# Turned rows of the last two blocks made in a pair's sixth step, for pairs 0 to 10

## Chip, cores and metric

The kernel runs on one core of one Trainium2 chip. The metric is the device time of one execution in microseconds; three runs of the kernel before gave 541.6, 541.94 and 542.74, median 541.94.

## What is computed

Attention over 4 batches, 8 heads, 576 positions and a head width of 64, with rotated queries and keys, and behind it a layer of 8 experts. Each position takes one expert: its own best one, or that of the position before it when a local gate says so. The reference, cut to its core:

```python
q_rot, k_rot = rotate(q), rotate(k)
scores = np.matmul(q_rot, k_rot.transpose(0, 1, 3, 2)) / np.sqrt(D)
attn = np.exp(scores - scores.max(-1, keepdims=True))
attn = attn / (attn.sum(-1, keepdims=True) + 1e-09)
x = np.matmul(attn, v).transpose(0, 2, 1, 3).reshape(B, S, H * D)
...
logits = x @ w_gate
local_gate = 1 / (1 + np.exp(-(x @ w_local)))
# e: argmax of the logits at s == 0 or local_gate < 0.5, else the expert of s - 1
h = np.maximum(x[b, s] @ w1[e], 0.0)
out[b, s] = softmax(logits[b, s])[e] * (h @ w2[e])
```

## The kernel before

The first 300 us are attention, the rest is the experts, which the change does not touch. Attention works on 16 pairs of heads (4 batches of 4 pairs), each in nine steps; the loop over `g` runs through 16 x 9 steps. In a step, DVE takes the minimum of a score tile (`mn`, L272), PE makes the scores of the next step (`s`, L267), ACT the exponentials (`e`, L289; the tile of the last 64 rows of both heads is `et`), PE turns the tile of two steps ago with four transposes (`tm`, L325; `tk` and `tt` are the remainders), and ACT and DVE split the turned tile into a high and a low part (`pth` L303, `ptl` L307). PE multiplies these with the split values (`pv`, L361, five matmuls in most steps, ten for a result), and ACT and DVE bring the result of a half out of PSUM (`tmp`, `xt`, L371 and L372). `xt` is the attention output of a pair with positions along the columns.

`gates(p)` turns that output of pair p into rows of positions, in the steps of pair p + 2. It gives a list of functions, one of which is called per step, from a list `soon`:

- `sums`: the row sums of the exponentials and their reciprocal (L426 to L429).
- `rows(0, 3)`: three `gx` matmuls (L435) turn blocks 0 to 2 and give the gate logits with them. For pairs 0 to 10 (`POOL_ROWS` is 11) ACT copies the result to SBUF (L442), and POOL divides logits (`gm`, L448) and rows (`xrow`, L449). The store waits in a list `stores`.
- `last_rows`: `rows(3, 2)` does two `gx` matmuls for the last two blocks, and DVE divides straight from PSUM (`gm`, `xrow`, the same L448 and L449) and stores at once (L459, L463). Behind it comes the store of `rows(0, 3)`.
- after the fourth pair of a batch, `scores`: three sums that make `lg_all` (L478 to L480), on POOL for the first three batches. From `lg_all` of the first three the routing starts with `mx` and `rs` on DVE (L500, L513).

`GATES_AT` says in which step of the pair this begins: step 7 unless it names the pair, so `sums` are in step 7, `rows(0, 3)` in step 8 and `last_rows` in step 0 of the next pair. Steps count from 0.

```python
GATES_AT = {13: 4, 14: 7, 15: 4}
...
                if i == GATES_AT.get(p, 7) and p >= 2:
                    soon += gates(p - 2)
...
                if soon:
                    soon.pop(0)()
```

`ps_t` is a pool of four PSUM banks that `tm`, `tk`, `tt`, `pv` and `gx` share. `et_p` is a pool of four SBUF buffers for `et` and `xrow`.

POOL has other work: it rotates queries and keys of pair p + 2 (`stage`, L196 and L197), splits them (`xq` and `xk`, L206 the high part, L207 the low part), and splits the values (`v`, L212 and L213). For every even pair `xq` is split at full width (1152 columns) with its keys in it; for an odd one `xk` and `xq` are apart, at 576. SP issues all loads and stores. In step 0 of a pair it issues the spread of the next pair's queries and keys, twelve DMAs from `xq` and `xk` (`qtail` L234, `m` L221 to L223, `qst` L229), then the load of raw queries and keys (L189), later the stores of `xrow` and the load of values (L193).

PE's instructions keep the order in which the program writes them, from step 12 on (`MAN0`), but the scheduler of the program decides the order on DVE, ACT, POOL and SP, and in six of the later pairs the order of PE that comes of all this differs by a few matmuls from that of the others.

Of the kernel before, what the change touches and what calls it, by code (L numbers as in the profile page):

```python
# [58 lines left out]
GATES_AT = {13: 4, 14: 7, 15: 4}  # L59

SPLITS = (((1, 2, 3, 4, 5, 7), (0, 6)), ((0, 1, 3, 5, 6, 7), (5, 6)), ((3, 4, 5, 6), (1, 5, 6)), ((1, 3, 4, 7), (1, 3, 4)), ((0, 2, 4, 5, 6), (5, 6)), ((3,), (0, 7)), ((2, 5, 6, 7), (4,)))
POOL_ROWS = 11
# [75 lines left out]
def tile_attention_moe(ctx, tc, qk, v, tabs, turn, consts, tri, wg, wts, out):  # L138
# [60 lines left out]
    def rope(p):  # L199
        for f in (1, 0):  # L200
            rope_half(pool, f, qkl[:, 2 * f:2 * f + 2])
# [34 lines left out]
    def spread(p):  # L236
        spread_tail(p)
        spread_k(p)
        spread_q(p)
# [9 lines left out]
    def mm_s(g):  # L249
        p, i = tile_of(g)  # L250
        m, q = m_t[p], qst[p % 2]
        st = ps_s.tile([P, 2, 512], F32, tag="s", name=f"s_{g}")
        whole = [(h, 0, HALF, h * HALF) for h in range(2)]

        turned = [(0, 0, HALF, 64), (1, 0, 224, 64 + HALF), (1, 224, HALF, 0)]
        if i < 8:
            a, j = heads_of(i, p)
            seq = [(q[:, a, j * P:(j + 1) * P], m[:, a, c], whole) for c in range(2)]
        elif p > 1:
            qt, k = qtail[p % 2], xk[p % 2]  # L260
            seq = [(qt[:, x], k[:, y], whole) for x, y in PASSES]
        else:
            seq = [(qtail0[p][:, a], m[:, a, c], (whole, turned)[a]) for a in range(2) for c in range(2)]
        for h in range(2):
            parts_ = [(lhs, keys, lo, hi, k0) for lhs, keys, parts in seq for hh, lo, hi, k0 in parts if hh == h]
            for n, (lhs, keys, lo, hi, k0) in enumerate(parts_):
                pe.matmul(st[:, h, lo:hi], lhs, keys[:, k0:k0 + hi - lo], start=(n == 0), stop=(n == len(parts_) - 1))  # L267
        s_t[g] = st

    def softmax_min(g):  # L270
        mn = sm_p.tile([P, 1], F32, tag="mn", name=f"mn_{g}", bufs=4)
        dve.tensor_reduce(mn, s_t[g][:, :, 0:HALF], axis=AX.XY, op=ALU.min)  # L272
        return mn

    def softmax_exp(g, mn):
        p, i = tile_of(g)
        b, hp = divmod(p, NP)
        sums = sum_t[b]
        if i < 8:
            a, j = heads_of(i, p)  # L280
            if a == 0:
                e_t[p, j] = ej_p.tile([P, 2, S], F32, tag="ej", name=f"e_{p}_{j}")
            dst = e_t[p, j][:, a]
            col = (2 * hp + a) * NB + j
        else:
            e_t[p, 4] = et_p.tile([P, S], F32, tag="et", name=f"et_{p}")
            dst = e_t[p, 4]
            col = (2 * hp + 1) * NB + 4
        act.activation(  # L289
            dst.rearrange("p (h s) -> p h s", h=2), s_t.pop(g)[:, :, 0:HALF], AF.Exp,  # L290
            bias=mn, scale=-1.0, accum_out=sums[:, col:col + 1],
        )
# [90 lines left out]
    def bc(ap, axis, n):  # L383
        ap = ap.unsqueeze(axis)
        shape = list(ap.shape)
        shape[axis] = n
        return ap.to_broadcast(shape)
# [3 lines left out]
    def small(shape, tag, dt=F32, bufs=1):  # L391
        return sm_p.tile(shape, dt, tag=tag, name=f"{tag}_{next(ctr)}", bufs=bufs)
# [24 lines left out]
    def gates(p):  # L417

        b, hp = divmod(p, NP)
        heads = slice(2 * hp, 2 * hp + 2)  # L420
        if hp == 0:
            gm_t[b] = small([P, NB, H, 9], "gm")
        r = sum_t[b].rearrange("p (h j) -> p h j", j=NB)[:, heads]

        def sums():
            act.copy(r[64:128, 0, 4:5], r[0:64, 1, 4:5])  # L426
            flat = sum_t[b][:, 2 * hp * NB:(2 * hp + 2) * NB]
            act.add(flat, flat, 1e-9)
            dve.reciprocal(flat, flat)  # L429

        def rows(j0, n):
            ps = ps_t.tile([P, n, 146], F32, tag="t", name=f"gx_{p}_{j0}")
            for j in range(j0, j0 + n):
                lo = j * P if j < 4 else S - P
                pe.matmul(ps[:, j - j0], xt_t[p][:, lo:lo + P], wid[:, hp // 2, 18 * (hp % 2):18 * (hp % 2) + 146],  # L435
                          start=True, stop=True)
            rj = r[:, :, j0:j0 + n].rearrange("p a j -> p j a")
            xr = et_p.tile([P, S], F32, tag="et", name=f"xrow_{p}_{j0}")
            o, w = ((18, 0), (0, 128))[hp % 2]
            if j0 == 0 and p < POOL_ROWS:  # L440
                xr = xr[:, 0:n * 146].rearrange("p (j d) -> p j d", d=146)
                act.copy(xr, ps)  # L442
                engine, ps, xr = pool, xr, xr[:, :, o:o + P]
            else:
                engine, xr = dve, xr[:, 0:n * P].rearrange("p (j d) -> p j d", d=P)
            px = ps[:, :, o:o + P].rearrange("p j (a d) -> p j a d", d=D)
            pw = ps[:, :, w:w + 18].rearrange("p j (a e) -> p j a e", e=9)
            engine.tensor_tensor(gm_t[b][:, j0:j0 + n, heads], pw, bc(rj, 3, 9), op=ALU.mult)  # L448
            engine.tensor_tensor(xr.rearrange("p j (a d) -> p j a d", d=D), px, bc(rj, 3, D), op=ALU.mult)  # L449
            if engine is pool:  # L450
                stores.append(lambda: store(j0, n, xr))
            else:
                store(j0, n, xr)

        def store(j0, n, xr):
            t0 = 1 + b * S
            cols = slice(P * hp, P * hp + P)
            m = min(j0 + n, 4) - j0
            sp.dma_start(rows_d[t0 + j0 * P:t0 + (j0 + m) * P, cols].rearrange("(j p) d -> p j d", p=P),  # L459
                         xr[:, 0:m])  # L460
            if m < n:

                sp.dma_start(rows_d[t0 + 4 * P:t0 + S, cols], xr[64:128, m])  # L463

        stores = []

        def last_rows():
            rows(3, 2)
            for f in stores:
                f()  # L470

        return [sums, lambda: rows(0, 3), last_rows]

    def scores(b):

# [718 lines left out]
    if True:  # L1194
# [32 lines left out]
        def pv_steps(t):  # L1227
            p, i = divmod(t, 9)
            if 0 <= p < NPAIR:
                for n in range(cum[i], cum[i + 1]):  # L1230
                    pv_mm(p, n)
                    if n % 10 == 9:
                        pv_evac(p, n // 10)

        for g in range(NSTEP):
            if g == GM:
                begin.close()
            with tc.manual_schedule(engines=None if g < GM else MAN0):
                p, i = divmod(g, 9)
                if i == 0 and p % NP == 0:  # L1240
                    b = p // NP
                    sum_t[b] = sm_p.tile([P, H * NB], F32, tag="sum", name=f"sum_{b}")
                    dve.memset(sum_t[b], 1.0)
                mn = minima.pop(g) if g in minima else softmax_min(g)
                if g == 0:
                    rest_q[0]()
                if g + 1 < NSTEP:
                    mm_s(g + 1)
                softmax_exp(g, mn)
                if g < GM - 1:  # L1250
                    minima[g + 1] = softmax_min(g + 1)
                if g >= 2:
                    tr_main(g - 2)
                pv_steps(g - 11)

                if i == 0 and 2 <= p and p + 2 < NPAIR or g == SPREAD_LAST:
                    spread(p + 1)
                if g in START:
                    for f in START[g]:
                        f()  # L1260
                if i == 0 and 1 <= p and p + 2 < NPAIR:
                    rope(p + 2)
                    if p + 3 < NPAIR:
                        load_qk(p + 3)
                if i == 5 and 1 <= p and p + 3 < NPAIR:
                    split_qk(p + 2)
                if g == QK_LAST:
                    split_qk(NPAIR - 1)
                if i == 3 and 1 <= p and p + 1 < NPAIR:
                    split_v(p + 1)  # L1270
                    if p + 2 < NPAIR:
                        load_v(p + 2)

                if i == GATES_AT.get(p, 7) and p >= 2:
                    soon += gates(p - 2)
                    if (p - 2) % NP == NP - 1:
                        soon.append(lambda b=(p - 2) // NP: scores(b))
                        if (p - 2) // NP == B - 2:
                            todo += route(0, B - 1)
                if soon:  # L1280
                    soon.pop(0)()
                f = todo.pop(0) if todo else None
                if f:
                    list(f())
# [106 lines left out]
```

## Time and profile before

| what | value |
|---|---|
| median of 3 runs | 541.94 us |
| the profiled execution | 541.58 us |
| its span | 539.7 us |
| busy: PE, DVE, ACT, POOL | 96%, 71%, 64%, 63% |
| granted TensorE clock, mean | 0.994 |

The profile comes from one execution. Its span runs from the first to the last instruction, its time has 1.88 us more around that. The busy shares are means over attention and experts, so they are read by stretches. A timeline row gives an instruction's start and length; a bracket behind it gives the idle time of its engine before it and what ended that. Instructions of one engine overlap a little at their ends, so what an instruction costs is read from the start of it to the start of the next.

### The profile page before, as it was taken

The page shows a single profiled execution, that of the slowest core. Times are in us where ns is not written, and L with a number is a line of the kernel's source. Part 1 is how long each engine was busy: PE and PEld are TensorE (multiplying, and loading weights), DVE is VectorE, ACT ScalarE, POOL GpSimd, SP SyncE. Part 2 cuts the span into 40 slices and gives each one's busy share as a digit, 9 for nine tenths or more (in the row PEclk, how much of TensorE's full clock was granted, in tenths as well). Part 3 has the DMA queues.
Part 4 walks back from the last instruction along what each step waited for, and adds up shares of the span by engine and source line. Part 5 has one row for each costly group of instructions (what it writes and reads, how often), then busy time and mean ns, then how long its engine had stood idle before and what let it go on. Part 6 is the DMA issues. An engine that isn't in the chain of part 4 may idle for free.

```text
span 539.7 us, 10708 instructions
## 1 busy us (share of the span) xinstructions
PE 517.0 (96%) x3273; PEld 458.5 (85%) x3273; DVE 381.9 (71%) x703; ACT 347.2 (64%) x762; POOL 341.3 (63%) x267
## 2 busy tenths in 40 slices
PE   7989999999999999998899999999999999999993
PEld 4889999999999999997888788887888888888882
DVE  6998999999999999999999935428422637421631
ACT  4988999999999999987676523353533443532440
POOL 4998989989969989896598302337511455411332
PEclk9999999999999999999999999999999999999997
DMA  8659698887886969977278205471637496637350
GB/s 275 279 132 230 183 246 231 209 192 216 217 229 134 233 189 235 223 189 171 39 200 230 83 20 177 125 267 49 225 103 238 125 353 151 203 100 234 84 172 26
DMA packets 63611, 97.37 MB, mean 180 GB/s; under 512 B 28146, under 2 KB 38898, under 8 KB 61747
## 3 DMA queue, kind: packets, MB, share of 16 engines
q1 hardware_dynamic: 60066, 86.48, 58.1%
q0 software_dynamic: 3040, 9.71, 5.6%
q8 instruction: 28, 0.46, 0.4%
q14 instruction: 45, 0.36, 0.2%
q10 hardware_dynamic: 432, 0.36, 0.2%
HBM read 76.98 MB, written 12.86 MB: 166 GB/s over the span
## 4 chain that ended last, share of the span: by engine, by line
PE 72%; DVE 10%; POOL 5%; DMA 4%; issue 4%; ACT 3%; SPq 1%; POOLq 0%; DVEq 0%; ACTq 0%
PE h L952 18%; PE o L995 17%; PE pv L361 12%; PE s L267 10%; PE tm L325 8%; DVE mn L272 3%; PE gx L435 2%; DVE ptl L307 2%; PE th L986 2%; DMA rows_d<-xrow 2%; PE tx L938 1%; POOL stage L196 1%; PE tk L335 1%; ACT e L289 1%; DMA qst<-xq 1%
## 5 line engine op out<-in xcount | busy, mean ns | idle before, releaser
L995 PE MATMUL o<-w,hs 128*128 128x512 f32 x456 | 112.9, 397 | 0.0
L272 DVE TENSOR_REDUCE mn<-s 128x1 f32<-128x576 f32 x144 | 107.2, 744 | 2.4 <-PE s L267 0.9
L952 PE MATMUL h<-w,xs 128*128 128x512 f32 x444 | 106.1, 392 | 0.8 <-DVE xs L307 0.5
L289 ACT ACTIVATE e<-s,mn 128x576 f32<-128x576 f32 x128 | 95.4, 746 | 14.8 <-DVE mn L272 12.0
L307 DVE TENSOR_TENSOR ptl<-tm,pth 128x512 fp32r<-128x512 f32 x139 | 95.3, 686 | 12.4 <-ACT pth L303 7.4
L1001 POOL DMA_INDIRECT out_dram<-os,sidx x19 | 23.1, 1214 | 123.6 <-ACTq L903 70.3
L267 PE MATMUL s<-m,qst 128*128 128x288 f32 x512 | 95.7, 309 | 4.5 <-ACT e L289 3.0
L952 PEld LDWEIGHTS h<-w,xs 128*128 128x128 f32 x444 | 82.5, 188 | 19.1 <-DVE w L897 1.1
L995 PEld LDWEIGHTS o<-w,hs 128*128 128x128 f32 x456 | 83.0, 188 | 16.9 <-DVE hs L307 0.4
L303 ACT CAST pth<-tm 128x512 fp32r<-128x512 f32 x139 | 80.9, 582 | 12.8 <-PE tm L325 11.8
L267 PEld LDWEIGHTS s<-m,qst 128*128 128x128 f32 x512 | 74.5, 188 | 8.4 <-ACT e L289 5.3
L361 PE MATMUL pv<-pth,v 128*128 128x288 f32 x256 | 76.8, 315 | 2.4 <-DVE pkl L307 1.3
L325 PE MATMUL tm<-wid,e 128*128 128x128 f32 x512 | 77.0, 272 | 0.6 <-ACT e L289 0.5
L361 PE MATMUL pv<-ptl,v 128*128 128x288 f32 x256 | 76.5, 314 | 0.0
L196 POOL TENSOR_TENSOR stage<-stage 128x1152 f32<-128x1152 f32 x26 | 69.1, 2667 | 4.4 <-DMA stage<-in_qk_dram 4.4
L325 PEld LDWEIGHTS tm<-wid,e 128*128 128x128 f32 x512 | 62.1, 140 | 1.2 <-ACT e L289 0.7
L897 DVE TENSOR_TENSOR w<-stage,w 128x1024 fp32r<-128x1024 f32 x37 | 51.0, 1412 | 15.6 <-ACT w L894 9.8
L361 PEld LDWEIGHTS pv<-pth,v 128*128 128x128 f32 x256 | 48.2, 188 | 6.0 <-issue 3.0
L361 PEld LDWEIGHTS pv<-ptl,v 128*128 128x128 f32 x256 | 48.3, 189 | 0.0
L307 DVE TENSOR_TENSOR xs<-tx,xs 128x512 fp32r<-128x512 f32 x19 | 13.1, 688 | 44.6 <-ACTq L903 35.0
L307 DVE TENSOR_TENSOR hs<-th,hs 128x512 fp32r<-128x512 f32 x26 | 17.5, 687 | 30.6 <-ACTq L903 18.9
L197 POOL TENSOR_TENSOR stage<-stage 128x576 f32<-128x576 f32 x26 | 37.0, 1430 | 0.3
(201 smaller groups left out, 821.4 us busy)
## 6 DMA issues: line engine op xcount, KB each, us to landing
stage<-in_wts_dram SPq DMA_DIRECT2D x84, 512.0 KB
stage<-in_qk_dram SPq DMA_DIRECT2D x13, 1152.0 KB
qst<-xq SPq DMA_DIRECT2D x56, 128.0 KB
stage<-in_v_dram SPq DMA_DIRECT2D x16, 320.0 KB
m<-xq SPq DMA_DIRECT2D x14, 288.0 KB
m<-xk SPq DMA_DIRECT2D x14, 288.0 KB
m<-xq SPq DMA_DIRECT2D x14, 256.0 KB
m<-xk SPq DMA_DIRECT2D x14, 256.0 KB
```

What stands on the lines that cost most here:

```text
L196: engine.tensor_tensor(x, x, tab[:, 2 * f:2 * f + 2], op=ALU.mult)
L197: engine.tensor_tensor(rr[:, f], x[:, 0], x[:, 1], op=ALU.add)
L267: pe.matmul(st[:, h, lo:hi], lhs, keys[:, k0:k0 + hi - lo], start=(n == 0), stop=(n == len(parts_) - 1))
L272: dve.tensor_reduce(mn, s_t[g][:, :, 0:HALF], axis=AX.XY, op=ALU.min)
L289: act.activation(dst.rearrange("p (h s) -> p h s", h=2), s_t.pop(g)[:, :, 0:HALF], AF.Exp, bias=mn, scale=-1.0, accum_out=sums[:, col:col ...
L303: act.copy(hi, src)
L307: dve.tensor_tensor(lo, src, hi.bitcast(F32), op=ALU.subtract)
L325: pe.transpose(ps[:, k], src[:, k * P:(k + 1) * P], ident)
L361: pe.matmul(pv_t[p, u], lhs.rearrange("p c d -> p (c d)"), rhs, start=(n == 0), stop=(n == 9))
L897: (pool if k in on_pool else dve).tensor_tensor(lo, src, hi.bitcast(F32), op=ALU.subtract)
L952: pe.matmul(ps[:, c], xs_t[t][:, x, k], w[y][:, c * 512:(c + 1) * 512], start=(k == 0 and n == 0), stop=(k == 3 and n == 2))
L995: pe.matmul(ps, hs_t[t][:, x, k], w[y][:, (k % 2) * 512:(k % 2 + 1) * 512], start=(k == 0 and n == 0), stop=(k == 7 and n == 2))
```

## The change

`gates(p)` for pairs 0 to 10 gives another list. It begins in step 4 and not in step 7: `sums` in step 4, `rows(3, 2)` with its stores in step 5, nothing in steps 6 and 7, `rows(0, 3)` in step 8 as before, and its store in step 0 of the next pair. For the last five pairs the list holds the same three parts as before, and `GATES_AT` names the step of pairs 13 to 15, which is where gates of pairs 11 to 13 begin. The lines behind the edit move up by two (L478 becomes L476, L500 becomes L498).

```diff
@@ -464,12 +464,10 @@
 
         stores = []
 
-        def last_rows():
-            rows(3, 2)
-            for f in stores:
-                f()
-
-        return [sums, lambda: rows(0, 3), last_rows]
+        if p < POOL_ROWS:
+            rest = lambda: None
+            return [sums, lambda: rows(3, 2), rest, rest, lambda: rows(0, 3), lambda: stores[0]()]
+        return [sums, lambda: rows(0, 3), lambda: rows(3, 2)]
 
     def scores(b):
 
@@ -1271,7 +1269,7 @@
                     if p + 2 < NPAIR:
                         load_v(p + 2)
 
-                if i == GATES_AT.get(p, 7) and p >= 2:
+                if i == GATES_AT.get(p, 4) and p >= 2:
                     soon += gates(p - 2)
                     if (p - 2) % NP == NP - 1:
                         soon.append(lambda b=(p - 2) // NP: scores(b))
```

Three places of the order in which the engines get their instructions. First PE, in steps 1 to 3 of a pair of the late six (numbers behind a name tell buffers and pairs apart). Before:

```order
L267 MATMUL s_2818<-m_2470,qst_100 128x288 x4
L325 MATMUL tm_2828<-wid,et_2740 128x128 x4
L341 MATMUL tt_2835<-wid,et_2740 128x128
L267 MATMUL s_2852<-m_2470,qst_100 128x288 x4
L361 MATMUL pv_0_2841<-pth_2537,v_8_2297 128x288
```

And now:

```order
L267 MATMUL s_2818<-m_2478,qst_100 128x288 x4
L325 MATMUL tm_2828<-wid,et_2748 128x128 x4
L341 MATMUL tt_2835<-wid,et_2748 128x128
L361 MATMUL pv_0_2841<-pth_2537,v_8_2297 128x288
L361 MATMUL pv_0_2841<-ptl_2538,v_8_2297 128x288
```

The four score matmuls stood in front of the five `pv` matmuls of the new result `pv_0`; now they stand behind them.

Second, DVE. Before, in steps 0 to 2 of the same pair:

```order
L307 TENSOR_TENSOR ptl_2538<-tm_2742,pth_2537 128x4x128
L448 TENSOR_TENSOR gm_2120<-gx_3_2773,sum_1285 128x2x18
L272 TENSOR_REDUCE mn_2816<-s_2787 128x1
L307 TENSOR_TENSOR ptl_2538<-tm_2794,pth_2537 128x4x128
L307 TENSOR_TENSOR pkl_2540<-tk_2801,pkh_2539 128x256
L272 TENSOR_REDUCE mn_2850<-s_2818 128x1
L449 TENSOR_TENSOR xrow_3_2776<-gx_3_2773,sum_1285 128x256
L372 TENSOR_TENSOR xt_2584<-pv_3_2749,tmp_2585 64x288
```

And now, the one piece in step 5 of the pair before it and the other in steps 0 to 2:

```order
L307 TENSOR_TENSOR ptl_2538<-tm_2631,pth_2537 128x4x128
L372 TENSOR_TENSOR xt_2584<-pv_1_2610,tmp_2585 64x288
L448 TENSOR_TENSOR gm_2037<-gx_3_2647,sum_1293 128x2x18
L449 TENSOR_TENSOR xrow_3_2650<-gx_3_2647,sum_1293 128x256
L272 TENSOR_REDUCE mn_2687<-s_2660 128x1
```

```order
L307 TENSOR_TENSOR ptl_2538<-tm_2750,pth_2537 128x4x128
L272 TENSOR_REDUCE mn_2816<-s_2787 128x1
L307 TENSOR_TENSOR ptl_2538<-tm_2794,pth_2537 128x4x128
L307 TENSOR_TENSOR pkl_2540<-tk_2801,pkh_2539 128x256
L272 TENSOR_REDUCE mn_2850<-s_2818 128x1
L372 TENSOR_TENSOR xt_2584<-pv_3_2757,tmp_2585 64x288
```

`gm` and `xrow` of the last two blocks stood five instructions apart; now they stand next to each other, behind an `xt` addition and ahead of `mn`.

Third, POOL, in the same pair, with the rotation before and the split of values behind. Before:

```order
L196 TENSOR_TENSOR stage<-stage 128x1152
L197 TENSOR_TENSOR stage<-stage 128x576
L206 TENSOR_SCALAR xq<-stage 128x1152
L448 TENSOR_TENSOR gm_2120<-xrow_0_2726,sum_1285 128x3x18
L449 TENSOR_TENSOR xrow_0_2726<-xrow_0_2726,sum_1285 128x3x128
L207 TENSOR_TENSOR xq<-stage,xq 128x1152
L212 TENSOR_SCALAR v_9_2588<-stage 128x10x64
```

And now:

```order
L196 TENSOR_TENSOR stage<-stage 128x1152 x2
L197 TENSOR_TENSOR stage<-stage 128x576 x2
L448 TENSOR_TENSOR gm_2037<-xrow_0_2734,sum_1293 128x3x18
L449 TENSOR_TENSOR xrow_0_2734<-xrow_0_2734,sum_1293 128x3x128
L206 TENSOR_SCALAR xq<-stage 128x1152
L207 TENSOR_TENSOR xq<-stage,xq 128x1152
L212 TENSOR_SCALAR v_9_2588<-stage 128x10x64
```

`gm` and `xrow` of blocks 0 to 2 stood between the two halves of the split of `xq`; now they stand ahead of both.

On SP, the two stores of the last two blocks stood directly behind the load of raw queries and keys; now they stand behind the load of values, ahead of the next spread.

## Rows read from the trace of the kernel before

**Rows 1.** The page: busy time by engine, and the chain that ended last by engine

```profile
PE 517.0 (96%) x3273; PEld 458.5 (85%) x3273; DVE 381.9 (71%) x703; ACT 347.2 (64%) x762; POOL 341.3 (63%) x267
...
PE 72%; DVE 10%; POOL 5%; DMA 4%; issue 4%; ACT 3%; SPq 1%; POOLq 0%; DVEq 0%; ACTq 0%
```

**Rows 2.** Windows: stretch and its length, busy PE, PEld, DVE, ACT, POOL, clock, DMA

```profile
120.00:140.00 20.00, 20.00 (x160) 19.80 (x159) 18.92 (x36) 18.62 (x47) 19.74 (x18) 1.00 0.74 191
160.00:180.00 20.00, 19.87 (x157) 19.29 (x156) 17.91 (x35) 18.21 (x47) 19.10 (x15) 1.00 0.68 177
240.00:260.00 20.00, 17.65 (x136) 16.32 (x135) 19.16 (x41) 14.95 (x36) 12.00 (x15) 1.00 0.72 163
```

**Rows 3.** Timeline of PE: start, length, what; brackets show idle time before

```profile
114.22 0.69 PE L267 MATMUL s<-m,qst 128*128 128x288 f32 x4
...
130.61 0.70 PE L267 MATMUL s<-m,qst 128*128 128x288 f32 x4
...
146.99 0.70 PE L267 MATMUL s<-m,qst 128*128 128x288 f32 x4
...
161.45 0.66 PE L435 MATMUL gx<-wid,xt 128*128 128x146 f32 x4
...
163.83 0.69 PE L267 MATMUL s<-m,qst 128*128 128x288 f32 x4
```

**Rows 4.** Waits of PE's weight loads, 145 to 245 us: total, times, longest

```profile
PEld pv L361 <- issue: 2.0, 6, 0.3
...
PEld tm L325 <- DVE ptl L307: 1.2, 6, 0.2
```

**Rows 5.** Timeline of DVE: two pairs

```profile
80.34 0.42 DVE L449 TENSOR_TENSOR xrow<-gx,sum 128x256 f32<-128x256 f32 x1 [0.57 <-DMA rows_d<-xrow]
...
162.75 0.18 DVE L448 TENSOR_TENSOR gm<-gx,sum 128x36 f32<-128x36 f32 x1
...
165.35 0.42 DVE L449 TENSOR_TENSOR xrow<-gx,sum 128x256 f32<-128x256 f32 x1
```

**Rows 6.** Timeline of PE: the first score matmuls of a pair

```profile
159.72 0.79 PE L267 MATMUL s<-m,qst 128*128 128x288 f32 x4
...
176.56 0.79 PE L267 MATMUL s<-m,qst 128*128 128x288 f32 x4
...
227.03 0.79 PE L267 MATMUL s<-m,qst 128*128 128x288 f32 x4
```

**Rows 7.** Timeline of POOL

```profile
160.62 0.29 POOL L448 TENSOR_TENSOR gm<-xrow,sum 128x54 f32<-128x54 f32 x1 [3.81 <-ACT xrow L442]
...
161.78 2.68 POOL L207 TENSOR_TENSOR xq<-stage,xq 128x1152 fp32r<-128x1152 f32 x1
...
191.83 1.16 POOL L206 TENSOR_SCALAR xq<-stage 128x1152 fp32r<-128x1152 f32 x1
...
227.93 0.28 POOL L448 TENSOR_TENSOR gm<-xrow,sum 128x54 f32<-128x54 f32 x1 [0.37 <-ACT xrow L442]
...
243.96 0.58 POOL L478 TENSOR_TENSOR gm<-gm 128x180 f32<-128x180 f32 x1
...
245.05 0.27 POOL L480 TENSOR_TENSOR lg_all<-gm 128x45 f32<-128x45 f32 x1
```

**Rows 8.** Timeline of SP's DMA issues

```profile
157.44 0.54 SPq L193 DMA_DIRECT2D stage<-in_v_dram  x1
164.49 1.58 SPq L234 DMA_DIRECT2D qtail<-xq  x2
```

**Rows 9.** DMA, 164 to 178 us in 40 slices: busy share in tenths

```profile
DMA  0000040133999989899998999999899940092795
```

**Rows 10.** Timeline of DVE where the routing begins

```profile
245.42 0.69 DVE L307 TENSOR_TENSOR ptl<-tm,pth 128x512 fp32r<-128x512 f32 x1 [0.34 <-ACT pth L303]
246.02 0.27 DVE L500 TENSOR_REDUCE mx<-lg_all 128x15 f32<-128x120 f32 x1
```

## Prediction

> **What bounds the kernel now.** I read the page first [rows 1]: PE is busy 96% of the span, and 72% of the chain that ended last is PE, but 10% is DVE, 5% POOL and 4% DMA, so somewhere the chain leaves PE. The windows [rows 2] say where. From 120 to 140 us PE is busy 20.00 of 20, from 160 to 180 it is busy 19.87, with POOL at 19.10, and from 240 to 260 only 17.65, with DVE at 19.16. So there are three regimes: attention bound by PE, attention in which PE has small holes and POOL is nearly full, and a stretch after 240 that DVE bounds.
>
> Next, the length of a pair. The timeline of PE [rows 3] gives the start of the same four score matmuls in successive pairs: 114.22 to 130.61 and on to 146.99 is 16.39 a pair, 146.99 to 163.83 is 16.84. The 0.45 us more is lost once per pair in the steps around these matmuls. The table of waits of 145 to 245 us [rows 4] counts six such pairs: PE waits for DVE ptl 0.2 six times, ahead of tm, and 0.3 with no releaser six times, ahead of pv. What DVE does there [rows 5] explains it: the two gx matmuls of blocks 3 and 4 start at 161.45, DVE reads them for gm at 162.75, but for xrow only at 165.35, until 165.77. For 4.3 us one of the four PSUM banks that tm, pv and gx share is not free, the next tm waits until ptl has emptied another, and the scheduler's order puts the scores of the next step in front of five pv matmuls. One earlier pair has another fault: xrow at 80.34 waited 0.57 us for a store out of its buffer, some 0.42 of which PE lost.
>
> **The change, part by part.**
>
> *Moved matmuls.* The two gx matmuls (four passes) leave the first step of the next pair for the sixth of the same one, eleven times. PE's work is the same. Cost on PE: nothing; the xt columns that they read were finished four steps earlier.
>
> *Moved DVE work.* gm and xrow (0.18 and 0.42, [rows 5]) now stand right behind the xt addition and in front of mn, and read their bank at once. DVE does as much as before per pair. Both engines get their extra work in the same step, so nothing is hidden or uncovered; what could be new is a bank that comes free late for tm in the step behind it. Bounds for that: 0, and the 0.2 of [rows 4] in each of eleven pairs, 2.2 in all; a gain there is excluded, since nothing is taken away from that step. I take 0, because the bank is held for the length of an xt, a gm and an xrow and not for 4.3 us.
>
> *The sums.* They are written down three steps earlier, but the order of ACT keeps them in their place and DVE's reciprocal moves by a few instructions: 0, within the step's other work.
>
> *The repair.* With xrow not in step 2, the order of PE in the six pairs is again tm, tt, five pv, scores, as it is in the pairs of 16.39. Gain: 6 x 0.45 = 2.7, and 0.42 for the pair at 80 us, whose xrow buffer is now stored a pair earlier: 3.1 us on PE.
>
> *POOL.* This is where I expect it to be paid back. In every second of the late pairs POOL splits xq at full width: L206, then L207, and the spread (SP's twelve DMAs that bring keys and queries of the next pair into place) starts when L207 is done: 161.78 + 2.68 = 164.46, issue at 164.49 [rows 7, 8]. Before, L206 ran while POOL would have waited for ACT's copy of the gx rows, and gm, xrow, L207 followed. In the new order gm and xrow stand in front of both halves. gm cannot start before 0.90 us after the pair's first scores S (160.62 against 159.72, [rows 6, 7]): it waited for ACT there, 3.81 us long. Then come gm and xrow, 1.16 (160.62 to 161.78), L206 at 1.16, L207 at 2.68, 0.03 to the issue. The spread thus starts at S + 5.93 where it started at S + 4.77.
>
> *From the spread to the next S.* Row 164.49 to the next S at 176.56 is 12.07 without a PE wait, so the data need at most 12.07. The DMA digits of 164 to 178 us (40 slices of 0.35 us) fall to 0 at the 34th, 175.55: at least 11.06 [rows 9]. So a full-width pair lasts at least 5.93 + 11.06 = 17.0 and at most 5.93 + 12.07 = 18.0 if that path binds, against 16.84 before and 16.39 on PE alone. I take the middle, 17.5. In the other pairs the split after gm is half as wide; by half of the rows (an estimate) the spread starts at 0.90 + 1.16 + 0.58 + 1.34 = S + 3.98, and the pair lasts 15.0 to 16.1: PE's 16.39 holds. In one of them the three sums for the routing (1.36, from 243.96 to 245.32, [rows 7]) come between L206 and L207: 16.4 to 17.4, middle 16.9.
>
> *The sum.* I count PE's lead over the kernel before, at the S of each pair. At 159.72 it is 0.42 + 0.45 = 0.87. A full-width pair: 16.84 - 17.5 = -0.66, lead 0.21. The pair with the sums: 16.84 - 16.9 = -0.06, lead 0.15. Full width: -0.51. Half width: +0.45, so at S = 227.03 the lead is -0.06. From there POOL decides: gm at 227.93 [rows 7] becomes 227.09 + 0.90 = 227.99, and L206, already done before, now follows it: L207 ends 0.06 + 1.16 = 1.22 later. POOL is then full up to lg_all, which ended at 245.32. DVE's mx, which reads it, started at 246.02, directly behind a ptl that began at 245.42 [rows 10], so there is up to 0.70 of room; behind it DVE is the bound for some 55 us (19.16 of 20). lg_all moves to 246.5, mx by 0.5 if all the room is there and by 1.2 if there is none. I take 0.5 to 0.6. The profiled execution lasted 541.58 (1.88 more than its span), which gives 542.1 to 542.2; the median of the runs, 541.94, is 0.36 above it, so **542.5 us**.
>
> *SP.* The two stores of blocks 3 and 4 now go behind the load of v and ahead of the next spread, where SP stood idle: its last issue there is at 157.44, the spread's first at 164.49 [rows 8]. The store of blocks 0 to 2 keeps its place. Cost 0, covered by those 7 us; without that cover two issues.
>
> *A rule against this.* The busiest engine in the windows is PE, in each of the first two of [rows 2]; POOL comes close only in the second. The Trainium skill (Perfetto Trace Analysis, Identifying the Most-Contended Engine) says to optimise the engine with the highest occupancy first. By that rule the holes of PE are the thing to close, POOL stays a follower, and the sum would be 541.94 - 3.1 = 538.8. The row at 160.62, where POOL waits 3.81 us, is for it; the new order on POOL is against.
>
> **The rivals.**
>
> *Faster: the repair carries through, 538.8 (up to 540.8 when part of it does).* Condition: the data arrive in 16.39 - 5.93 = 10.5 us or less, or POOL catches up elsewhere, and mx is reached as early as PE is. For it: six equal holes, with a cause that the change removes. Against: the DMA digits show the queues full until 11.06. At 11.06 itself the pairs last 17.0, 16.4, 17.0 and 16.4, the lead at 227.03 is 1.4, L207 ends 0.3 earlier, and the end gains between 0.3 and 1.0: still hardly outside 0.2%. Chance 0.2.
>
> *Slower: POOL and the spread set the pair, 543.0 to 544.6.* Mechanism: gm waits for ACT in front of the whole split, and the data land late. At 12.07 the full-width pairs last 18.0, the pair with the sums 17.4, the lead at 227.03 is -1.6, L207 ends 2.7 later and mx 2.0 to 2.7, which makes 543.9 to 544.6. It decides from some 11.76 us to landing on: then POOL is 1.8 late and mx 1.1. For it: no wait of PE shows that the data were early at 176.56. Against: nothing shows that they were late. Chance 0.32.
>
> *No change at all: the chain after 226 us is POOL, then DVE, and PE's holes lie beside it.* It gives 541.9, which lies inside the forecast's own range of 541.0 to 543.0.
>
> **How the numbers follow.** A measurement of this kernel tells some 0.2%, 1.1 us, from no change. The forecast, repair paid back by POOL's order, has 0.48 with the inert case in it, faster 0.2, slower 0.32. The range reaches down to 540.0, where about half of the faster case is left out, and up to 544.0, past the middle of the slower case.
>
> **What would show it.** Right: pairs of 16.39 on PE between 147 and 165 us, the order pv before scores, no PE wait on ptl there; then pairs alternating between about 17.5 and 16.4 with new PE waits ahead of the first scores of a pair, released by the qst transfers; on POOL gm still waiting for ACT, xq behind it; lg_all about a us later, mx with it. Wrong: equal pairs of 16.39 up to 227 us and lg_all 2 us earlier (the rule), or tm waiting for ptl in the seventh step of eleven pairs (the bank), or mx more than 2 us late.

## The result, and the profile after

The changed kernel took 545.63 us (median of 6, 544.73 to 545.92), the kernel before 542.18 in the runs beside it (median of 6). The ratio is 1.0056, with an interval of 1.0045 to 1.0067: slower by 3.0 us, 2.4 to 3.6 (the two medians differ by 3.45). The forecast was 542.5, its range 540.0 to 544.0.

The page's head and engine line of the changed kernel, profiled in a run of 545.75:

```profile
span 543.9 us, 10718 instructions
...
PE 519.2 (95%) x3273; PEld 460.3 (85%) x3273; DVE 379.6 (70%) x703; ACT 347.3 (64%) x762; POOL 341.6 (63%) x267
```

The work is that of [rows 1]; the span is 4.2 us longer (543.9 against 539.7).

Windows of the changed kernel, columns as in [rows 2]:

```profile
120.00:140.00 20.00, 19.22 (x150) 18.41 (x149) 17.50 (x33) 17.44 (x44) 18.57 (x15) 1.00 0.70 187
160.00:180.00 20.00, 19.72 (x155) 19.14 (x154) 17.04 (x33) 18.58 (x47) 17.77 (x14) 1.00 0.72 195
240.00:260.00 20.00, 16.71 (x119) 15.92 (x118) 16.81 (x37) 13.64 (x35) 15.00 (x15) 0.91 0.76 173
```

PE had 20.00 from 120 to 140 us in [rows 2] and has 19.22 now, 19.87 from 160 to 180 and 19.72 now, and 17.65 from 240 to 260, where 16.71 is left and DVE, which was the bound there at 19.16, falls to 16.81. Three waits of DVE from 60 to 250 us (total, times, longest) that the kernel before does not have:

```profile
DVE sum L1241 <- POOL xrow L449: 2.4, 2, 2.0
DVE mx L498 <- POOL lg_all L478: 1.5, 1, 1.5
DVE gm L448 <- POOL lg_all L478: 1.4, 1, 1.4
```

**Where the three microseconds lie.** The first scores S of a pair on PE, in the changed kernel:

```profile
60.62 0.79 PE L267 MATMUL s<-m,qst 128*128 128x288 f32 x4
...
110.08 0.79 PE L267 MATMUL s<-m,qst 128*128 128x288 f32 x4
...
127.85 0.79 PE L267 MATMUL s<-m,qst 128*128 128x288 f32 x4
...
160.88 0.79 PE L267 MATMUL s<-m,qst 128*128 128x288 f32 x4
...
177.99 0.77 PE L267 MATMUL s<-m,qst 128*128 128x288 f32 x4 [0.24 <-DMA qst<-xq]
...
196.24 0.77 PE L267 MATMUL s<-m,qst 128*128 128x288 f32 x4 [0.40 <-ACT pth L303]
...
212.62 0.78 PE L267 MATMUL s<-m,qst 128*128 128x288 f32 x4
...
229.22 0.79 PE L267 MATMUL s<-m,qst 128*128 128x288 f32 x4
...
246.75 0.78 PE L267 MATMUL s<-m,qst 128*128 128x288 f32 x4 [0.68 <-DMA qst<-xq]
```

and the first of these in the kernel before:

```profile
60.52 0.79 PE L267 MATMUL s<-m,qst 128*128 128x288 f32 x4
```

With the rows at 159.72 and 227.03 of [rows 6] and mx at 246.02 of [rows 10], and mx of the changed kernel, on DVE,

```profile
249.10 0.28 DVE L498 TENSOR_REDUCE mx<-lg_all 128x15 f32<-128x120 f32 x1 [1.54 <-POOL lg_all L478]
```

the way from that first S to mx has three pieces, none of which gained:

| piece | before | now | change |
|---|---|---|---|
| six pairs, up to S near 160 | 159.72 - 60.52 = 99.20 | 160.88 - 60.62 = 100.26 | +1.06 |
| four pairs, up to S near 228 | 227.03 - 159.72 = 67.31 | 229.22 - 160.88 = 68.34 | +1.03 |
| from there to mx | 246.02 - 227.03 = 18.99 | 249.10 - 229.22 = 19.88 | +0.89 |

Together 2.98, the 3.0 of the ratio. Behind mx the delay is handed on: the next mx, that of the last batch, follows the first by 57.25 us before (303.27 - 246.02) and by 57.46 now (306.56 - 249.10). What lies between mx and the end of the span differs by another 1.1 in these two executions (294.80 against 293.68), but by 2.2 between those of experiments 2 and 11 further on (294.85 and 292.60), so nothing is read from it.

**The six pairs.** One of them, 110.08 to 127.85, lasts 17.77; the other five average (100.26 - 17.77) / 5 = 16.50. The timelines of DVE, POOL and PE show what happens in the long one:

```profile
123.70 0.20 DVE L448 TENSOR_TENSOR gm<-gx,sum 128x36 f32<-128x36 f32 x1 [1.44 <-POOL lg_all L478]
```

```profile
123.38 0.28 POOL L478 TENSOR_TENSOR lg_all<-gm 128x45 f32<-128x45 f32 x1
```

```profile
124.37 0.63 PE L325 MATMUL tm<-wid,e 128*128 128x128 f32 x4 [0.58 <-DVE xrow L449]
```

DVE's gm of the last two blocks of a new batch waits 1.44 us for POOL's lg_all of the batch before. `gm_t` has one buffer for all batches (`small` gives one by default), so nobody may write the new batch's logits before POOL has summed the old ones. Before, POOL's own gm was the first to write it, behind the sums on the same engine. Now DVE is first. While it waits, the gx result holds its PSUM bank, and tm waits 0.58 for DVE's xrow, which frees it. DVE's next mn, behind xrow, is late too: ACT's e waits 1.71 us for it, and PE's scores at 125.86 wait for that e. PE loses 17.77 - 16.50 = 1.27.

**The four pairs and the end.** POOL and SP:

```profile
161.82 0.28 POOL L448 TENSOR_TENSOR gm<-xrow,sum 128x54 f32<-128x54 f32 x1 [3.19 <-ACT xrow L442]
...
162.99 1.15 POOL L206 TENSOR_SCALAR xq<-stage 128x1152 fp32r<-128x1152 f32 x1
...
164.23 2.67 POOL L207 TENSOR_TENSOR xq<-stage,xq 128x1152 fp32r<-128x1152 f32 x1
...
230.16 0.28 POOL L448 TENSOR_TENSOR gm<-xrow,sum 128x54 f32<-128x54 f32 x1 [2.40 <-ACT xrow L442]
...
232.56 2.69 POOL L207 TENSOR_TENSOR xq<-stage,xq 128x1152 fp32r<-128x1152 f32 x1
...
248.80 0.27 POOL L478 TENSOR_TENSOR lg_all<-gm 128x45 f32<-128x45 f32 x1
```

```profile
166.92 1.46 SPq L234 DMA_DIRECT2D qtail<-xq  x2
...
183.92 1.28 SPq L234 DMA_DIRECT2D qtail<-xq  x2
...
235.28 1.28 SPq L234 DMA_DIRECT2D qtail<-xq  x2
```

The row at 161.82 answers to the one at 160.62 in [rows 7]: gm starts 0.94 behind S and waits for ACT as before, but L206 and L207 now stand behind it (162.99, 164.23). The spread starts at 166.92, which is S + 6.04, and the scores at 177.99 wait 0.24 for the qst transfer, 11.07 after the spread's start. That pair lasts 17.11. In the next one the sums for the routing come between the halves of the split; its spread starts at 183.92 (S + 5.93), the pair lasts 18.25, and the next S comes 12.32 after the spread. PE waits twice in it: 0.54 for e at 182.27, behind the memset that holds DVE for 2.0 us, and 0.40 at its end, where the profile names ACT's pth, though that ended at 195.87; what PE waited for there is not settled. The last of the four, 212.62 to 229.22, lasts 16.60, and the pair behind it 17.53, with a wait for qst again, of 0.68, 11.47 after the spread's start at 235.28. At the end gm stands at S + 0.94 and L207 at S + 3.34 (232.56), where [rows 7] have them at S + 0.90 and S + 2.06 (227.93, and 1.16 later by their own distance of 160.62 to 161.78). lg_all and mx are late by that, and DVE stands idle for 1.54 where in [rows 10] mx followed a ptl without a wait.

### The profile page after: what moved, and what is told of

Same layout as the page of the kernel before. It is cut to its first block, busy times and chain, and to the rows that moved or that the text cites. A ratio compares the mean times of both kernels' runs of the same rounds, so it can differ in the third digit from the quotient of the medians.

```text
span 543.9 us, 10718 instructions
## 1 busy us (share of the span) xinstructions
PE 519.2 (95%) x3273; PEld 460.3 (85%) x3273; DVE 379.6 (70%) x703; ACT 347.3 (64%) x762; POOL 341.6 (63%) x267
## 5 line engine op out<-in xcount | busy, mean ns | idle before, releaser
L307 DVE TENSOR_TENSOR hs<-th,hs 128x512 fp32r<-128x512 f32 x26 | 17.5, 687 | 30.8 <-ACTq L901 19.1
```

The source lines that it names most:

```text
L307: dve.tensor_tensor(lo, src, hi.bitcast(F32), op=ALU.subtract)
```

## Experiments

The theory from these rows: three new costs, (a) DVE's wait for the single gm buffer, (b) POOL's order, gm and xrow ahead of the split, and (c) a memset of `sum`, which the scheduler now places earlier on DVE and which waits 2.0 us at 178 us for a buffer (in the waits above). The rivals: only the buffers, or only POOL's order.

**1. gm of the second batch in a buffer of its own.** No buffer space was left, so the 360 columns lie in a part of `ohr`, a tile that is first needed later. The order of all engines is that of the changed kernel.

```diff
-            gm_t[b] = small([P, NB, H, 9], "gm")
+            gm_t[b] = small([P, NB, H, 9], "gm") if b != 1 else <360 free columns of ohr>
```

> The changed kernel, but the logits gm of the second batch lie in a buffer of their own, so that DVE's first gm of that batch waits for nobody. Theory (three new costs in the changed kernel: DVE's wait for lg_all at 122 us, POOL's gm ahead of the split of xq in the late pairs, a memset of sum that waits at 178 us; what is lost early is passed on): the wait of 1.44 us is gone, the pair from 113.7 to 131.5 falls from 17.77 to about 16.5, every later pair starts about 1.3 us earlier, and the time falls by 1.0 to 1.4, to some 544.4. Rival (the wait doesn't matter, since POOL and the spread set the late pairs by themselves): the wait is gone but the starts after 178 us stay, and the time is 545.6, within 0.3.

Measured: 545.16 us, ratio to the kernel before 1.006 (1.0037 to 1.0084). The interval takes in both expectations, so the time doesn't tell them apart. The profile does: the wait is gone, that pair lasts 16.52 (111.15 to 127.67), and mx comes 248.62 - 61.65 = 186.97 after the first S, where it came 249.10 - 60.62 = 188.48 after it, 1.5 later. DVE still waits there, on POOL:

```profile
248.62 0.28 DVE L498 TENSOR_REDUCE mx<-lg_all 128x15 f32<-128x120 f32 x1 [0.89 <-POOL lg_all L478]
```

**2. POOL's order.** gm and xrow of blocks 0 to 2 are tied behind the last instruction of `split_qk`. PE's order is that of the changed kernel; on DVE the memset of (c) changes its place and no longer waits 2.0 us.

```diff
-            pool.tensor_tensor(x[:, 1], src, x[:, 0].bitcast(F32), op=ALU.subtract)
+            last_split[0] = pool.tensor_tensor(x[:, 1], src, x[:, 0].bitcast(F32), op=ALU.subtract)
...
+            with tc.issue_after(last_split[0].ins) if engine is pool else ExitStack():
-            engine.tensor_tensor(gm_t[b][:, j0:j0 + n, heads], pw, bc(rj, 3, 9), op=ALU.mult)
...
```

> The changed kernel, but POOL must issue gm and xrow of blocks 0 to 2 behind the split of xq in its order; nothing else differs but the place of one memset. Theory: the spreads of the late pairs start 1.2 to 3 us earlier after the first scores, the pairs that lasted 17.1 to 18.3 fall to 16.4 to 16.7, and lg_all and mx come about 2 to 3 us earlier; time 542.0 to 543.2, that is most of the loss. Rival (what is lost lies in the waits of DVE for buffers, not in POOL's order): time within 0.5 of 545.6. Rival (gm only moves the wait: lg_all, now behind the whole split, comes as late as before): PE's pairs shorten, lg_all stays near 249, time 545.

Measured: 541.39 us, ratio 0.9996 (0.9982 to 1.0011). The whole loss is gone; 542.0 to 543.2 was expected. POOL, PE and DVE of this run (line numbers are two or three higher):

```profile
159.75 1.16 POOL L206 TENSOR_SCALAR xq<-stage 128x1152 fp32r<-128x1152 f32 x1
...
163.62 0.29 POOL L451 TENSOR_TENSOR gm<-xrow,sum 128x54 f32<-128x54 f32 x1
...
245.82 0.28 POOL L481 TENSOR_TENSOR lg_all<-gm 128x45 f32<-128x45 f32 x1
```

```profile
61.66 0.79 PE L269 MATMUL s<-m,qst 128*128 128x288 f32 x4
...
161.93 0.79 PE L269 MATMUL s<-m,qst 128*128 128x288 f32 x4
...
228.37 0.79 PE L269 MATMUL s<-m,qst 128*128 128x288 f32 x4
```

```profile
246.65 0.27 DVE L501 TENSOR_REDUCE mx<-lg_all 128x15 f32<-128x120 f32 x1
```

The split runs in the time that POOL spent waiting for ACT, from 159.75, and gm follows at 163.62 without a wait. The four late pairs last (228.37 - 161.93) / 4 = 16.61, lg_all comes at 245.82, that is 184.16 after the first S and four us earlier than in the changed kernel (248.80 - 60.62 = 188.18), and no pair waits for qst. The long pair is still there, from 111.11 to 128.90, 17.79.

**3. sum of the second batch in a buffer of its own.**

```diff
-                    sum_t[b] = sm_p.tile([P, H * NB], F32, tag="sum", name=f"sum_{b}")
+                    sum_t[b] = sm_p.tile(...) if b != 1 else <40 free columns of ohr>
```

> The changed kernel, but the row sums of the second batch lie in a buffer of their own, so that the memset for the last batch waits for nobody. Theory: DVE's wait of 2.0 us at 178 us is gone, but the pair from 178 to 196 is set by POOL and the spread, so it stays at 17.5 or longer; time 545.1 to 545.6. Rival (the memset is what makes that pair 18.3 long): the pair falls to 17 or less and the time by 1 or more, to 544.6 or less.

Measured: 545.49 us, ratio 1.007 (1.0047 to 1.0094). The wait of 2.0 us is gone from the profile. The pair from 178.85 to 196.52 lasts 17.67 for 18.25, as theory had it, but the one ahead of it 17.29 for 17.11, and mx comes 249.37 - 61.24 = 188.13 after the first S for 188.48. So (c) is worth 0.35 at the most; the rest was covered by the wait at the end of the pair, which has grown from 0.40 to 1.05.

**4. All three edits together.**

> The changed kernel with all three: gm and sum of the second batch in buffers of their own, and POOL's gm and xrow behind the split of xq. Theory: the repair of the six late pairs is then kept; all pairs from 64 to 230 us last 16.4 to 16.6, lg_all ends at 244 or earlier, and the time is 539.5 to 541.2, faster than the kernel before. Rival (DVE bounds the stretch after 240 us and takes back what PE gains): PE gains 2 us by 230 us, but mx starts no earlier than 245.5, and the time is 541.8 to 542.5.

Measured: 540.03 us, ratio 0.9966 (0.9952 to 0.9981): faster than both kernels. S on PE, and mx:

```profile
61.31 0.79 PE L269 MATMUL s<-m,qst 128*128 128x288 f32 x4
...
160.34 0.79 PE L269 MATMUL s<-m,qst 128*128 128x288 f32 x4
...
226.78 0.79 PE L269 MATMUL s<-m,qst 128*128 128x288 f32 x4
```

```profile
245.08 0.27 DVE L501 TENSOR_REDUCE mx<-lg_all 128x15 f32<-128x120 f32 x1
```

The three pieces of the way to mx are 99.03, 66.44 and 18.30: shorter than in the kernel before by 0.17, 0.87 and 0.69, together 1.73, and the medians differ by 1.83 (541.86 in the runs beside it).

**5. POOL's order alone, in the kernel before.** The edit of experiment 2 on the kernel before; only five L207 change places.

> The kernel before, with the one edit on POOL: gm and xrow of blocks 0 to 2 are issued behind the split of xq, as in the run with POOL's order; all other engines keep their order. Theory (in the kernel before, the data of the next pair came just in time, so an earlier spread gains nothing, and PE's late pairs stay at 16.8 us by their own order): 541.4 to 542.3, no difference. Rival (POOL's order bounds the kernel before too): 540.9 or less, late pairs shorter than 16.8.

Measured: 541.76 us, ratio 0.9998 (0.9983 to 1.0013). The kernel before loses nothing to its own order.

**6. The other way round: the changed kernel's order in the kernel before.** In pairs 8, 10 and 12 `split_qk` is called behind `rows(0, 3)` and tied behind its xrow. On all engines only three L206 move.

```diff
+            with tc.issue_after(last_gm[0].ins) if p - 2 in SWAP else ExitStack():
...
+    SWAP, last_gm = (8, 10, 12), [None]
...
-                if i == 5 and 1 <= p and p + 3 < NPAIR:
+                if i == 5 and 1 <= p and p + 3 < NPAIR and p not in SWAP:
                     split_qk(p + 2)
...
+                if i == 8 and p in SWAP:
+                    split_qk(p + 2)
```

> The kernel before, with nothing changed but three places on POOL: in the three late pairs with a split at full width, L206 goes behind gm and xrow, which is the order of the changed kernel. Theory: gm still starts 0.9 us after the pair's first scores, the spread 1.2 us later than before, the three pairs take 17.1 to 17.6 where they took 16.8, lg_all and mx come 1.5 to 2.5 us later; time 543.3 to 544.4. Rival (the order alone was covered; the loss needs PE's shorter pairs or DVE's waits): 541.9 within 0.5.

Measured: 543.84 us, ratio 1.0052 (1.0039 to 1.0065), nearly the whole loss of the change by the medians, with nothing of the change in it. The profiled run was the lowest of its five, 541.91; its POOL and PE show the mechanism all the same:

```profile
159.68 0.28 POOL L451 TENSOR_TENSOR gm<-xrow,sum 128x54 f32<-128x54 f32 x1 [5.20 <-ACT xrow L445]
...
162.08 2.66 POOL L208 TENSOR_TENSOR xq<-stage,xq 128x1152 fp32r<-128x1152 f32 x1
```

```profile
158.78 0.79 PE L270 MATMUL s<-m,qst 128*128 128x288 f32 x4
...
176.32 0.77 PE L270 MATMUL s<-m,qst 128*128 128x288 f32 x4 [0.45 <-DMA qst<-xq]
```

gm waits 5.20 us, L207 (here L208) starts at 162.08 behind it, the pair lasts 17.54, and its last wait is for qst. The trace shows less than the medians do: the second full-width pair, 193.12 to 209.99, lasts only 16.87, a half-width one behind it, to 227.64, lasts 17.65 for a reason that the order of POOL does not give, and mx comes 246.62 - 59.99 = 186.63 after the first S, 1.13 later than before (246.02 - 60.52 = 185.50; 1.5 to 2.5 was expected). So the cost of the order is shown by the times of all five runs, and its way through POOL and qst by one pair of the fastest run.

**7. The bank freed early, the matmuls in their old place.** The kernel before with the order of experiment 2, and DVE's next mn tied behind xrow of the last two blocks.

```diff
+        with tc.issue_after(last_x[0].ins) if last_x[0] else ExitStack():
             dve.tensor_reduce(mn, s_t[g][:, :, 0:HALF], axis=AX.XY, op=ALU.min)
```

> The kernel before, with the gx matmuls of blocks 3 and 4 in their old place, but DVE must issue the next mn behind xrow, so that their PSUM bank is free after half a microsecond, and POOL's gm behind the split as in the run beside it. PE's order in the six late pairs is then pv before scores again. Theory (the bank held for 4.3 us cost 0.45 us in each of six pairs): late pairs 16.4 to 16.6, time 539.3 to 540.9, 1 to 2.5 below the run with the order alone. Rival (the pairs were long for another reason): pairs of 16.8, time 541.9 within 0.5.

Measured: 549.01 us, ratio 1.015 (1.0135 to 1.0164). Both expectations missed: PE's waits of this run, from 60 to 245 us, say why.

```profile
PE s L269 <- ACT e L295: 11.2, 13, 1.3
```

PE's order is repaired: the two steps in question take, in a late pair, 171.71 - 168.23 = 3.48, as in an early pair of the kernel before (117.69 - 114.22 = 3.47), where a late one takes 167.76 - 163.83 = 3.93. But mn is on the chain to the exponentials, and tied behind gm and xrow it comes late in all pairs: PE waits for ACT's e thirteen times, 0.6 to 1.3. The tie cost more than the bank; the run shows the repair in these two steps and tells nothing of what it is worth in the time of the kernel.

**8. The last two blocks in step 4.** Experiment 4 with `GATES_AT.get(p, 3)` and one more empty step ahead of `rows(0, 3)`.

> All three edits on the changed kernel as in the run of that name, and the two gx matmuls, gm and xrow of blocks 3 and 4 one step earlier, in step 4, where DVE has no xt addition. Theory (the pairs of 16.5 where the kernel before had 16.4 come from DVE having xt, gm and xrow in one step): the wait of pv for ptl of 0.17 us goes in eleven pairs, pairs 16.4, time 538.6 to 539.6. Rival (that wait comes from elsewhere): pairs 16.5, 540.0 within 0.5.

Measured: 540.67 us, ratio 0.9977 (0.9955 to 1.0), 0.17 above the rival's range. In its mechanism the rival holds: the pairs last 16.48 to 16.60, and the wait of 0.17 for ptl is still there once in each of eleven pairs.

That wait is not what makes the pairs longer. The kernel before has it too, in early pairs that last 16.39:

```profile
118.75 0.19 PEld L361 LDWEIGHTS pv<-pth,v 128*128 128x128 f32 x1 [0.17 <-DVE ptl L307]
```

What is new is a second one, ahead of the first pv of the new result, just behind tt. DVE's pkl of the tile tk and PE's weight load for that pv, in an early pair of the kernel before, and in an early and a late pair of the changed kernel:

```profile
114.76 0.41 DVE L307 TENSOR_TENSOR pkl<-tk,pkh 128x256 fp32r<-128x256 f32 x1
...
115.29 0.19 PEld L361 LDWEIGHTS pv<-pth,v 128*128 128x128 f32 x1
```

```profile
114.35 0.41 DVE L307 TENSOR_TENSOR pkl<-tk,pkh 128x256 fp32r<-128x256 f32 x1
...
114.88 0.19 PEld L361 LDWEIGHTS pv<-pth,v 128*128 128x128 f32 x1 [0.18 <-issue]
...
165.21 0.41 DVE L307 TENSOR_TENSOR pkl<-tk,pkh 128x256 fp32r<-128x256 f32 x1
...
165.74 0.19 PEld L361 LDWEIGHTS pv<-pth,v 128*128 128x128 f32 x1 [0.24 <-issue]
```

The load starts 0.12 after pkl ends in each of the three, and 0.11 to 0.13 after it in all eleven pairs of experiments 4 and 8. Without the two gx matmuls in the first step of the pair, PE has loaded tt at 114.69, S + 4.61, where it was at 115.22, S + 5.09 (S is 110.08 and 110.13): 0.48 sooner. DVE's pkl ends only 0.36 sooner (S + 4.68 for S + 5.04), and in the late pair 0.30 sooner (165.62, S + 4.74). So the weight loads pause there for 0.07 us in an early pair of the kernel before, and in experiments 4 and 8 for 0.15 to 0.20 in the six pairs up to 160 us and for 0.23 to 0.26 behind them. That is about what the pairs of 16.50, and most of what those of 16.61, have above 16.39. The profile names no releaser that holds for all of them, and no run moves pkl alone, so this is read from the times and not shown by an experiment. It fits that step 4 is no better than step 5 for the two blocks: the step that they left is the same.

**9. and 10. The new list for the late pairs alone**, from pair 5 on, with POOL's order tied (9) and left to the scheduler (10).

```diff
+        if p < 5:
+            return [sums, lambda: rows(0, 3), last_rows]
         if p < POOL_ROWS:
...
-                if i == GATES_AT.get(p, 4) and p >= 2:
+                if i == GATES_AT.get(p, 4 if p > 6 else 7) and p >= 2:
```

> The new list only for pairs 5 to 10, that is for the six late pairs; pairs 0 to 4 keep the list of the kernel before; POOL's gm and xrow behind the split. No buffers are added. Theory: the pairs up to 147 us last 16.4 (but for the one at 81 us, whose store may be awaited again), there is no wait for lg_all at 122 us, the late pairs last 16.6, lg_all ends at about 244; time 539.4 to 540.6, faster than the kernel before and like the run with all three edits. Rival (the early pairs need the new list too, or the second batch's logits are awaited all the same): 541.3 or more.

> The new list only for pairs 5 to 10, as in the run beside it, but POOL's order is left to the scheduler, which puts gm and xrow ahead of the split of xq in the later pairs. Theory: the wait at 122 us is gone and yet the late pairs with a split at full width last 17 to 18 us again; time 543.0 to 545.0. Rival (the wait for lg_all at 122 us was the larger part): 541.0 to 542.5.

Measured: 542.06 us, ratio 1.0004 (0.9987 to 1.002), and 545.45 us, ratio 1.0071 (1.0044 to 1.0098). Both are slower than expected (539.4 to 540.6, and 543.0 to 545.0). The ninth shows why:

```profile
149.40 0.80 PE L269 MATMUL s<-m,qst 128*128 128x288 f32 x4 [0.79 <-ACT e L291]
```

Where the lists change over, a pair takes 18.35, from the third scores of one pair at 131.05 to the third of the next at 149.40, with waits of 0.75 and 0.79 for e at its end. Two sets of last blocks fall into that stretch (gx at 137.93) or just ahead of it (128.69); ACT there has its e behind a pth that waits for PE's tm (0.44 and 1.32 us). That the one made the other is not shown. The same pair stands in the tenth run (waits of 0.76 and 0.79), so neither prices the late pairs by itself. The distance between the two, 0.0067 or 3.6 us (3.4 by the medians), is POOL's order again, without any wait of DVE for lg_all at 122 us in either.

**11. POOL's order and gm apart, sum as it was.**

> The changed kernel with POOL's gm and xrow behind the split and gm of the second batch in a buffer of its own; sum stays as it was. Theory: once POOL no longer sets the late pairs, the wait of 1.44 us at 122 us costs its 1.3 us in full, so the time is 1.0 to 1.6 below the run with POOL's order alone, 539.9 to 540.5, the same as with all three. Rival (the buffer of the sums brought that gain): as with POOL's order alone, 541.4 within 0.5.

Measured: 540.18 us, ratio 0.998 (0.9964 to 0.9997). The first S on PE, and mx:

```profile
60.70 0.79 PE L269 MATMUL s<-m,qst 128*128 128x288 f32 x4
```

```profile
244.40 0.27 DVE L501 TENSOR_REDUCE mx<-lg_all 128x15 f32<-128x120 f32 x1
```

The pair from 110.18 to 126.72 lasts 16.54 where experiment 2 had 17.79, and mx comes 244.40 - 60.70 = 183.70 after the first S; in experiment 2 it came 246.65 - 61.66 = 184.99 after it, 1.29 later. So the wait of the single buffer, (a), is paid in full at mx, with POOL's order right or not. The ratios differ by 0.0016, some 0.9 us, in the same sense, though their intervals overlap (the two profiled runs are the highest of twelve in experiment 2 and the lowest of twelve here, so nothing is read from their own times). Experiment 4, which has sum apart as well, has 183.77: (c) has no part in it here either.

## Why the prediction was wrong

It named a mechanism that made the kernel slower, priced it about right, and put the time three microseconds too low, because the lead that it set against that mechanism was a loss, from waits that it had not looked for.

- *The sum* failed at its first number, a lead of 0.87 at the first late S. Measured: -1.06, an error of 1.93, of which 1.27 is the wait for the gm buffer and 0.66 the six pairs at 16.50 for 16.39. The second piece was forecast from a lead of 0.87 to -0.06, a loss of 0.93, and measured 1.03. The third was forecast as 0.5 to 0.6 in all, the lead of -0.06 in it, and is 0.89. At mx the forecast was thus 0.5 to 0.6 late, and 2.98 was measured.
- *POOL* and *From the spread to the next S* were right in the mechanism, and nearly in size. In the first full-width pair the spread came at S + 6.04 for S + 5.93, and data 11.07 after its start, at the low end of 11.06 to 12.07. Which pair is long was wrong: the one with the sums took 18.25 for 16.9, with its spread at S + 5.93 for 3.98 + 1.36 = S + 5.34 and the next S 12.32 after it, above the 12.07; the full-width one behind it took 16.38 for 17.5, with its spread at 201.63, S + 5.39. That the four pairs together take 68.34, where the forecast's 17.5, 16.9, 17.5 and 16.39 make 68.29, is luck in that these two errors cancel. At the end L207 was to come 1.16 later than S, and comes 3.34 - 2.06 = 1.28 later.
- The step that failed is *Moved DVE work*, a term taken as 0 with 2.2 us as its bound. It asked whether the PSUM bank comes free in time, and bounded that by 0.2 a pair; it did not ask who else writes gm. The change makes DVE the first writer of a new batch's logits, in a tile with one buffer whose reader, lg_all, stood far back on POOL: 1.27 us at one place. The question about the bank had the right sense all the same, as tm waits there for the bank that the waiting gm holds. Its sentence "nothing is hidden or uncovered" failed as well: it looked at the step that gets the work and not at the one that loses it, where PE now comes to the new pv sooner than DVE's pkl (experiment 8), 0.11 in each of the six pairs up to 160 us and some 0.2 in each behind them.
- *The repair* was oversized. The late pairs fell from 16.84 to 16.6 and not to 16.39, even with POOL's order set right (16.61 in experiments 2 and 4), and the early ones rose from 16.39 to 16.5. Experiment 4, with neither of the two losses, gains 0.17 in the six pairs where the forecast had 0.87. The 0.42 for the pair at 80 us is not a cost of every execution either: the same pair lasts 16.40 and 16.39 in experiments 5 and 6, with the old list.
- The memset that moved and waited 2.0 us was not foreseen, and cost 0.35 at the most (experiment 3).
- *The rule* of the Trainium skill (Perfetto Trace Analysis, Identifying the Most-Contended Engine) would have given 538.8. For TensorE that section of the Trainium skill goes by MFU (the share of peak FLOP/s that is used) and the busy share of weight loads; PEld, 19.29 of 20 us from 160 to 180 in [rows 2], leads there as well. The runs disagree: PE is the busiest engine in all of these kernels, and yet three L206 moved on POOL, at PE's unchanged work, changed the time by 2.8 us (experiment 6, 0.0052 of 542), while PE's own holes were worth 1.7 at the most (experiment 4).
- The rival *Slower* had the mechanism, but was priced from the lead of 0.87 too. It came nearest in time (545.6, a us above its 544.6), but without its condition: where PE waited for qst by the profile, the data landed 11.07 and 11.47 after the spread's start, below its 11.76. What took the time past its end is the loss ahead of 160 us, which it did not have.

## What to carry to other kernels

A step moved by a line of the program is moved on every engine by the scheduler, and the place where it costs may be an engine that the change doesn't mention: compare the order of all engines, look for an instruction that now waits at the head of a queue, and tie what must not stand behind it. Look also at the step that the work leaves: an engine that is done sooner there may wait for another that is not. Before moving a write to another engine or an earlier step, look up how many buffers its tile has and where the last reader of the old content stands. Here the change is worth 1 to 2 us when both are put right (experiments 4 and 11), and costs 3 when neither is.

## What the runs showed beside that

The granted clock of TensorE fell after the stall that stands behind the late mx (PE waits 2.50 us for e, until 252.99). Windows of the changed kernel around it, columns as above:

```profile
250.00:252.00 2.00, 0.49 (x4) 0.25 (x2) 1.98 (x3) 0.78 (x2) 1.26 (x1) 1.00 0.09 22
...
254.00:256.00 2.00, 1.89 (x10) 1.69 (x8) 1.64 (x5) 1.91 (x5) 2.00 (x3) 0.55 0.92 214
```

PE was busy 0.49 of 2 us, and two stretches later the granted clock is 0.55, near its lower level of 1.2 GHz, where 1.00 is 2.4 GHz. A stall of this kind need not bring it: in experiment 10 PE was busy 0.51 us from 250 to 252 and 1.16 in the next two, 1.01 in the changed kernel, and the clock stayed at 1.00. No run here prices the fall by itself.
